# Tile starts rounded to 256 bytes, an earlier first unit, and a per-unit norm with its root on GpSimd

## The chip, the core and the metric

One core of a Trainium2 chip runs the program. TensorE (PE in the profile) multiplies matrices and loads its weights under the row name PEld; VectorE is DVE, ScalarE is ACT, GpSimd is POOL, and SyncE (SP) issues most transfers. The metric is device time in microseconds (us), the median of several executions.

## The reference, cut to what matters

```
for c in range(nc):                      # 24 chunks of 32 positions
    L = exp(cum[:, :, :, None] - cum[:, :, None, :]) * causal
    y[:, :, sl] = einsum(M = CB * L, xc) + einsum(Cc, state) * exp(cum)
    state = decay_full * state + sum(Bx)
x = y as 3072 tokens x 256
xn = x / sqrt(mean(x * x) + 1e-6) * rms_g
x = (silu(xn @ w_gate) * (xn @ w_val)) @ w_out      # 256 -> 1536 -> 256
return softplus(x @ w_in) @ w_out2                  # 256 -> 2048 -> 256
```

A decaying scan over the sequence (4 batches, 8 heads) is followed by a norm and two MLP layers, all in float32.

## The kernel before, in words

The 3072 tokens are 24 units of 128 tokens, and four units make one of six blocks of 512 tokens. A **unit** is the scan part: the decay factors of its tokens are spread over partitions, DVE scans them (line 502), PE makes scores (`a<-hw` in the first eight units), DVE multiplies the two (line 549), PE makes the unit's output (`t<-xc`, `t<-ab,xc`), and ACT stores its square and its copy scaled by `rms_g` in the tiles `xxh` and `xxl`. For the first four units the spread is two matmuls for each half of a unit, with the identity as weights (`p<-Sm,ident`; `Sm` there holds the clipped factors); later units fetch a spread copy by DMA (`ab<-a_clip`). The **norm** of a block sums squares on PE (`p<-mean,xxh`), takes the inverse root on DVE by three Newton steps (lines 628 to 637), spreads it over partitions on PE (`p<-ident,rs`), multiplies on DVE (line 656), and splits the product into a float32r high part (ACT, line 299) and a rest (DVE, line 306). `NORMS = {0: [3, 1]}` says that block 0 does this for units 0 to 2 together and for unit 3 alone.

The **MLP** then takes each product in three passes, high weight by high input, high by rest and rest by high, with 512 columns a matmul. Layer 1 has F1 = 12 tiles of 128 and 18 matmuls in each, layer 2 has F2 = 16 tiles and 12 in each, so a block takes 12 x 18 + 16 x 12 = 408 such matmuls and the six blocks 2448. Their weights (`wgh` to `wpl`) stay in SBUF; their moving operand is in an `xx` tile, an `hw` tile, or, for the first two tiles of layer 1 in blocks 3 to 5 (`EARLY`), in a `wr` tile. Weights arrive in 34 chunks in three `wr` buffers and are turned into pairs by ACT and DVE (lines 386 to 393); the first three chunks are issued on ACT's queue, the others on SP's.

**Fillers** are 40 matmuls of a constant (`p<-mean`, both operands read with a step of zero) that do no work for the result. Eight of them come first by rank, and 32 have the last rank of all, so they stand wherever the planner sees PE idle.

The order of each engine is set by `Plan.emit`: every operation has a rank, an estimated duration and its dependences, and the planner picks at each step the operation that can start first, by rank among equals. An engine then runs its instructions in that order, and an instruction that waits holds up those behind it.

SBUF tiles are placed one behind another, in steps of 32 bytes. Because `cst_sb` has 257 columns and `wr` has 1025, the starts are not multiples of 256 bytes. In the built program the start modulo 256 is 224 for all ten weight tiles; 64 for `xx`, `hw`, `s`, `ab` and `xc`; 192 for `cz` and `st`; and 224, 0 and 32 for the three `wr` buffers.

Of the kernel before, what the change touches and what calls it, by code (L numbers as in the profile page):

```python
# [17 lines left out]
P = 128  # L18
# [6 lines left out]
BLOCKS = [4, 4, 4, 4, 4, 4]  # L25

NATIVE, SPREAD = 8, 4
NORMS = {0: [3, 1]}

EARLY, HEAD = 2, 2  # L30

# [203 lines left out]
def tile_ssd_then_swiglu_then_softplus_mlp(  # L235
# [75 lines left out]
        plan.op({"sp": (kb * 4.0, fn)}, rank, r, w)  # L311


    cst_sb = const.tile([P, DM + 1], F32, name="cst_sb")
    ident4 = const.tile([P, 4 * P], F32, name="ident4")
    ident = ident4[:, 0:P]
    mask = cst_sb[:, 0:DM]
    zeros = cst_sb[:, DM:DM + 1].to_broadcast([P, P])
    g_sb = const.tile([P, KD], F32, name="g_sb")
    cz = [const.tile([P, 4, 2, P], F32, name=f"cz{i}") for i in range(2)]  # L320
    mean = const.tile([P, 1], F32, name="mean")
    zz = [const.tile([P, 4 * P], F32, name=f"zz{i}") for i in range(2)]


# [42 lines left out]
    def weight(c):  # L367
        nm, i = chunks[c]
        b0 = blocks[0]
        use = b0["t1"] + 2 * i * b0["d1"] if nm in ("wg", "wv", "wo") else b0["t2"] + 2 * i * b0["d2"]  # L370
        if nm in ("wo", "wp"):
            use += 2.0
        rank = use - W_LEAD

        raw = buf("wr", [P, 8 * P + 1], I32, N_W)
        mid = lambda: raw()[:, 1:].rearrange("p (n j) -> p n j", j=2)[:, :, 0]
        r = lambda: mid().bitcast(F32)

        plan.op({"actq" if c < N_W else "sp": (512 * 4.0, lambda: (act if c < N_W else nc.sync).dma_start(
            out=raw().bitcast(U16)[:, 1:-1], in_=w[c].bitcast(U16)))}, -150 + c if c < N_W else rank, (), [raw])  # L380
        n = 2 * KD * P

        z, zk = zz[c % 2], ("zz", c % 2)
        ACT(n, rank, lambda: act.activation(out=z.bitcast(F16).rearrange("p (n j) -> p n j", j=2)[:, :, 1],
            in_=raw().bitcast(BF16)[:, 2:].rearrange("p (n j) -> p n j", j=4)[:, :, 2], func=ACTF.Copy, scale=0.5), [raw], [zk])
        DVE(n, rank, lambda: dve.scalar_tensor_tensor(out=mid(), in0=mid(), scalar=13, in1=z.bitcast(I32),  # L388
            op0=ALU.logical_shift_right, op1=ALU.bitwise_or), [raw, zk], [raw])
# [12 lines left out]
        COPY(n, rank, lambda: l, gp, [gp], [(nm, i, 1)], False)
# [20 lines left out]
    def split(t):  # L423
        rank = base_of(NB * t) - B_LEAD
        for q in range(2):
            hl = buf("wr", [P, 8 * P + 1], I32, N_W)
            hi, lo = (lambda hl=hl, k=k: f32(hl()[:, 4 * P * k:4 * P * (k + 1)]) for k in range(2))
            LOAD(256, rank, lambda q=q, lo=lo: nc.sync.dma_start(out=lo(), in_=bc[t, :, q]), [hl])
            ACT(512, rank, lambda hi=hi, lo=lo: act.activation(out=hi().bitcast(F32R), in_=lo(), func=ACTF.Copy), [hl], [(hl, 0)])
            DVE(512, rank, lambda hi=hi, lo=lo: dve.tensor_tensor(out=lo().bitcast(F32R), in0=lo(), in1=hi(), op=ALU.subtract),  # L430
                [hl, (hl, 0)], [hl])
            for i, (p, k, sl) in enumerate(((hi, (hl, 0), slice(0, 4, 2)), (lo, hl, slice(1, 4, 2))) if q == 0 else
                                           ((hi, (hl, 0), slice(0, 2)), (lo, hl, slice(2, 4)))):
                LOAD(512, rank, lambda p=p, q=q, sl=sl: nc.sync.dma_start(
                    out=parts[t][q][:, sl], in_=p().rearrange("p (o f) -> p o f", o=1).to_broadcast([P, 2, 4 * P])),
                    [("parts", t, 2 * q + i)], [k])

    def unit(u):
# [87 lines left out]
        if nat:  # L526

            def scores():
                for q in range(4):
                    c = slice(q * P, (q + 1) * P)  # L530
                    for z in range(2):
                        rows = slice(r0 + 64 * z, r0 + 64 * z + NS)
                        mm(gps[z]()[:, c], bct()[rows, 0, c], bct()[rows, 1, c], True, True)
            PE(1100, rank[0], scores, [(bct, b % 2, 0), (bct, b % 2, 1)], list(gps), 512)
        else:
            def pairs():
                for q in range(4):
# [73 lines left out]
    def norm(t, o0, nu, rank, step):  # L611

        c = slice(o0 * P, (o0 + nu) * P)
        sq, y, r0 = ysq[t]
        ss, rs = buf("ss", [P, 4], F32, 2), buf("rs", [P, 2, 4], F32, 2)
        nb = pbuf("a" if t else "p", [P, 4 * P])

        def msum():
# [2 lines left out]
                    mm(nb()[:, o:o + 1], sq()[:, k, (o0 + o) * P:(o0 + o + 1) * P], mean, k == 0, k == KD - 1)  # L621
        PE(230 * KD * nu, rank, msum, [(sq, o0 + o) for o in range(nu)] + ["mean"], [nb], 8)

        def root():


            r, q, m = rs()[:, 0, 0:nu], rs()[:, 1, 0:nu], ss()[:, 0:nu]
            dve.tensor_scalar(out=m, in0=nb()[:, 0:nu], scalar1=1e-6, scalar2=0.5, op0=ALU.add, op1=ALU.mult)
            dve.tensor_scalar(out=r.bitcast(I32), in0=m.bitcast(I32), scalar1=-0.5, scalar2=float(0x5F3759DF - 2 ** 22 - 2 ** 31),
                              op0=ALU.mult, op1=ALU.add)  # L630
            for _ in range(3):
                if nu == 1:
                    dve.scalar_tensor_tensor(out=q, in0=r, scalar=r, in1=m, op0=ALU.mult, op1=ALU.mult)
                else:
                    dve.tensor_tensor(out=q, in0=r, in1=r, op=ALU.mult)
                    dve.tensor_tensor(out=q, in0=q, in1=m, op=ALU.mult)
                dve.scalar_tensor_tensor(out=r, in0=q, scalar=1.5, in1=r, op0=ALU.subtract, op1=ALU.mult)
        DVE(0, rank + step, root, [nb, "mean"], [rs, ss], port=False, ns=(8 if nu == 1 else 11) * 185)

        def spread():  # L640
            for o in range(nu):
                mm(nb()[:, o * P:(o + 1) * P], rs()[:, 0, o:o + 1].to_broadcast([P, P]), ident, True, True)
        PE(240 * nu, rank + step, spread, [rs, "ident"], [nb], 512 * nu)
        if not o0:
            xnT[t] = [buf(f"xx{k}", [P, KD, 4 * P], F32R, 3) for k in "hl"]
# [3 lines left out]
            h.rank = l.rank = r0 + 0.01  # L649

        for ks in ([slice(0, KD)] if nu < 4 else [slice(k, k + 1) for k in range(KD)]):
            m = ks.stop - ks.start
            n = m * nu * P
            yk = [(y, k, o0 + o) for o in range(nu) for k in range(ks.start, ks.stop)]
            hv, lv, yv = (lambda b=b, ks=ks: b()[:, ks, c] for b in (h, l, y))
            DVE(n, rank + 2 * step, lambda yv=yv, m=m: dve.tensor_tensor(out=yv(), in0=yv(), in1=nb()[:, 0:nu * P].rearrange(
                "p (o i) -> p o i", o=1).to_broadcast([P, m, nu * P]), op=ALU.mult), yk + [nb], yk, port=False)
            COPY(n, rank + 2 * step, hv, yv, yk, [(h, o0, ks.start)])
            REST(n, rank + 2 * step, lv, yv, hv, yk + [(h, o0, ks.start)], [(l, o0, ks.start)])
            xkeys.setdefault(t, []).extend([(h, o0, ks.start), (l, o0, ks.start)])  # L660
# [16 lines left out]

    def split_h(key, s, n, rank, early=False):
        if early:
            hhl = buf("wr", [P, 8 * P + 1], I32, N_W)  # L680
            hhl.view = lambda t: t[:, 0:8 * P].bitcast(F32R).rearrange("p (s i) -> p s i", s=2)
        else:
            hhl = buf("hw", [P, 2, 4 * P], F32R, N_H)
# [72 lines left out]
    with tc.manual_schedule():  # L756
# [14 lines left out]
        LOAD(96, -101, lambda: nc.sync.dma_start(out=a_sb(), in_=a_view(ab)), [a_sb])  # L771
        DVE(384, -101, clip_all, [a_sb], [a_sb])
        LOAD(96, -101, lambda: nc.sync.dma_start(out=a_view(a_clip), in_=a_sb()), ["a_clip"], [a_sb])
        LOAD(128, -10, lambda: nc.sync.dma_start(out=cst_sb, in_=cst), ["cst"], ["a_clip"])
        LOAD(20, -1, lambda: nc.sync.dma_start(out=g_sb, in_=rms_g), ["g"])
        DVE(1, -104, lambda: dve.memset(mean, 1.0 / DM), (), ["mean"])
        for i in range(2):
            POOL(500, -103, lambda i=i: pool.memset(zz[i], 0.0), (), [("zz", i)])
        for i in range(2):
# [111 lines left out]
```

## Time and profile before

| what | value |
|---|---|
| median of 3 runs | 677.12 us (676.54 to 677.94) |
| time of the profiled execution | 677.4 us |
| its span, first to last instruction | 675.5 us |
| PE busy | 665.6 us, 99% |
| DVE busy | 343.9 us, 51% |
| ACT busy | 308.4 us, 46% |
| POOL busy | 20.6 us, 3% |

A busy PE is not a PE at its peak, because matmuls overlap and the end of each is modelled; the distance from one start to the next tells more. Some 1.9 us of the execution lie outside the span.

### The profile page before, as it was taken

How to read it: one execution, taken by the hardware profiler on the slowest of the kernel's cores; microseconds unless marked ns; L12 is line 12 of the kernel's file. 1: busy time of each engine (PE TensorE's matmuls, PEld its weight loads, DVE VectorE, ACT ScalarE, POOL GpSimd, SP SyncE). 2: the span in 40 equal slices, each digit the busy share in tenths (PEclk: the TensorE clock that was granted, in tenths of full speed). 3: DMA queues.
4: the chain of work that ended last, by engine and by line, in shares of the span. 5: the costliest groups of instructions: out<-in, count | busy, mean ns of one | idle time of the engine just before them, and what ended most of it. 6: DMA issues, size and time to landing. Idle time of an engine off the chain costs nothing.

```text
span 675.5 us, 9002 instructions
## 1 busy us (share of the span) xinstructions
PE 665.6 (99%) x3492; PEld 533.5 (79%) x3492; DVE 343.9 (51%) x580; ACT 308.4 (46%) x541; POOL 20.6 (3%) x28
## 2 busy tenths in 40 slices
PE   7999999999999999999999999999999999999997
PEld 5677788888888888888888888888888888887785
DVE  2969898785862226763423873433653422233321
ACT  3247756775444445332644432544432544422543
POOL 1000000000000000000000100000100000000000
PEclk9989999999999999999999999999999999999999
DMA  6746677555620006120231620040500000000000
GB/s 200 212 128 224 228 264 233 202 188 175 190 57 32 0 1 190 57 67 0 83 120 37 210 67 1 30 167 7 194 1 1 0 1 0 32 0 1 0 1 31
DMA packets 36777, 61.36 MB, mean 91 GB/s; under 512 B 3424, under 2 KB 18304, under 8 KB 36736
## 3 DMA queue, kind: packets, MB, share of 16 engines
q1 hardware_dynamic: 36304, 59.23, 27.0%
q10 hardware_dynamic: 432, 1.57, 0.7%
q8 instruction: 27, 0.44, 0.3%
q14 instruction: 14, 0.11, 0.1%
HBM read 47.58 MB, written 13.21 MB: 90 GB/s over the span
## 4 chain that ended last, share of the span: by engine, by line
PE 95%; DMA 2%; DVE 1%; issue 1%; ACT 0%; SPq 0%; DVEq 0%
PE p L268 52%; PE t L268 35%; PE a L268 7%; DMA ab<-a_clip 1%; DMA hw<-in_bc 1%; DVE ab L502 0%; DVE hw L306 0%; ACT hw L299 0%; DVE ab L549 0%; DVE xxh L549 0%; DVE s L793 0%; DVE xxl L746 0%; DVE s L705 0%; DVE wr L388 0%; ACT s L717 0%
## 5 line engine op out<-in xcount | busy, mean ns | idle before, releaser
L306 DVE TENSOR_TENSOR hw<-s,hw 128x512 fp32r<-128x512 f32 x162 | 113.4, 702 | 187.3 <-ACT hw L299 186.8
L299 ACT ACTIVATE hw<-s 128x512 fp32r<-128x512 f32 x162 | 101.8, 631 | 113.7 <-DVE s L705 87.1
L268 PE MATMUL t<-hw,wph 128*128 128x512 f32 x384 | 121.2, 396 | 0.2 <-DVE hw L306 0.2
L717 ACT ACTIVATE s<-p 128x512 f32<-128x512 f32 x96 | 57.0, 599 | 109.0 <-PE p L268 108.1
L705 DVE TENSOR_TENSOR s<-s,p 128x512 f32<-128x512 f32 x72 | 49.2, 684 | 79.8 <-PE p L268 71.2
L268 PEld LDWEIGHTS t<-hw,wph 128*128 128x128 f32 x384 | 71.3, 188 | 19.0 <-issue 1.2
L268 PE MATMUL t<-hw,woh 128*128 128x512 f32 x264 | 83.6, 397 | 0.3 <-DVE hw L306 0.2
L268 PE MATMUL p<-xxh,wil 128*128 128x512 f32 x192 | 76.5, 399 | 0.0
L268 PE MATMUL t<-hw,wpl 128*128 128x512 f32 x192 | 76.5, 398 | 0.0
L268 PE MATMUL p<-xxl,wih 128*128 128x512 f32 x192 | 75.8, 395 | 0.2 <-DVE xxl L746 0.2
L268 PE MATMUL p<-xxh,wih 128*128 128x512 f32 x192 | 75.5, 393 | 0.0
L701 ACT ACTIVATE s<-p 128x512 f32<-128x512 f32 x72 | 43.0, 597 | 57.3 <-PE p L268 56.5
L268 PEld LDWEIGHTS t<-hw,woh 128*128 128x128 f32 x264 | 49.0, 188 | 13.2 <-ACT hw L299 0.6
L268 PE MATMUL p<-xxh,wgh 128*128 128x512 f32 x144 | 57.5, 399 | 0.0
L268 PE MATMUL p<-xxh,wvl 128*128 128x512 f32 x144 | 57.3, 398 | 0.0
L268 PE MATMUL p<-xxh,wgl 128*128 128x512 f32 x144 | 57.2, 398 | 0.0
L268 PE MATMUL p<-xxh,wvh 128*128 128x512 f32 x144 | 57.1, 397 | 0.0
L268 PE MATMUL p<-xxl,wgh 128*128 128x512 f32 x144 | 56.9, 395 | 0.0
L268 PE MATMUL p<-xxl,wvh 128*128 128x512 f32 x144 | 56.8, 395 | 0.0
L502 DVE TENSOR_TENSOR_SCAN ab<-ab,ident 128x512 f32<-128x512 f32 x40 | 50.3, 1277 | 5.1 <-DMA ab<-a_clip 4.9
L268 PE MATMUL t<-hw,wol 128*128 128x512 f32 x132 | 52.5, 398 | 0.0
L268 PEld LDWEIGHTS p<-xxl,wih 128*128 128x128 f32 x192 | 36.0, 188 | 9.7 <-DVE xxl L746 0.7
(120 smaller groups left out, 791.3 us busy)
## 6 DMA issues: line engine op xcount, KB each, us to landing
wr<-in_w SPq DMA_DIRECT2D x31, 512.0 KB, 3.3
ab<-a_clip SPq DMA_DIRECT2D x20, 512.0 KB, 4.2
parts<-wr SPq DMA_DIRECT2D x16, 512.0 KB, 3.5
xc<-in_xc SPq DMA_DIRECT2D x20, 256.0 KB, 4.2
st<-parts SPq DMA_DIRECT2D x16, 256.0 KB, 3.3
cz<-parts SPq DMA_DIRECT2D x32, 128.0 KB, 3.6
out_y<-s SPq DMA_DIRECT2D x12, 256.0 KB, 3.8
wr<-in_bc SPq DMA_DIRECT2D x8, 256.0 KB, 3.0
```

Source lines behind the costliest of these rows:

```text
L268: pe.matmul(out=o, lhsT=l, rhs=r, start=start, stop=stop, skip_group_check=True)
L299: ways = {"act": (act_ns(n), lambda: act.activation(out=out(), in_=in_(), func=ACTF.Copy)), "dve": (dve_ns(n, sbuf), lambda: dve.tensor_co ...
L306: return lambda: eng.tensor_tensor(out=out(), in0=in_(), in1=f32(hi()), op=ALU.subtract)
L502: DVE(512, rank[0], lambda t=t, d=d: dve.tensor_tensor_scan(out=t(), data0=d(), data1=ident4, initial=0.0, op0=ALU.mult, op1=ALU.add), dk ...
L701: ACT(n, rank - EPI, lambda: act.activation(out=s()[:, 0:n], in_=ps[0]()[:, 0:n], func=ACTF.Silu), [ps[0]], [s, "table"] if new_table else ...
L705: DVE(n, rank - EPI, lambda: dve.tensor_tensor(out=s()[:, 0:n], in0=s()[:, 0:n], in1=ps[1]()[:, 0:n], op=ALU.mult), [s, ps[1]], [s], port= ...
L717: ACT(n, rank - EPI, lambda: act.activation(out=s()[:, 0:n], in_=hp()[:, 0:n], func=ACTF.Softplus), [hp], [s, "table"] if new_table and f ...
```

## The change

Four things are changed. (1) Tiles get sizes that keep every large tile's start at a multiple of 256 bytes: `cst_sb` is padded, the small constants share a tile or get 64 columns, and `wr` has 8P + 64 columns in place of 8P + 1. In the built program the start modulo 256 is 0 for every tile of weights, `xx`, `hw`, `wr`, `s`, `ab`, `xc`, `cz` and `st`. (2) The first three weight loads depend on `ident`, so that ACT issues them behind its first copies. (3) The scores of the first four units depend on `a_sb`, the clipped factors. (4) The norm of block 0 goes unit by unit, and its root is one ACT copy that adds 1e-6 and one power of -0.5 on POOL in place of the Newton steps on DVE; the other blocks keep the Newton steps.

```diff
-NORMS = {0: [3, 1]}
+NORMS = {0: [1, 1, 1, 1]}
...
-    cst_sb = const.tile([P, DM + 1], F32, name="cst_sb")
+    sbuf_at = 1152
+    cst_sb = const.tile([P, -(-(sbuf_at // 4 + DM + 1) // 64) * 64 - sbuf_at // 4], F32, name="cst_sb")
...
-    g_sb = const.tile([P, KD], F32, name="g_sb")
+    small = const.tile([P, 64], F32, name="small")
+    g_sb, mhalf = small[:, 0:KD], small[:, KD:KD + 1]
+    mean = const.tile([P, 64], F32, name="mean")[:, 0:1]
...
-    mean = const.tile([P, 1], F32, name="mean")
...
-        raw = buf("wr", [P, 8 * P + 1], I32, N_W)
+        raw = buf("wr", [P, 8 * P + 64], I32, N_W)
...
-            out=raw().bitcast(U16)[:, 1:-1], in_=w[c].bitcast(U16)))}, -150 + c if c < N_W else rank, (), [raw])
+            out=raw().bitcast(U16)[:, 1:16 * P + 1], in_=w[c].bitcast(U16)))}, -150 + c if c < N_W else rank, ["ident"] * (c < N_W), [raw])
...
-            PE(1100, rank[0], scores, [(bct, b % 2, 0), (bct, b % 2, 1)], list(gps), 512)
+            PE(1100, rank[0], scores, [(bct, b % 2, 0), (bct, b % 2, 1)] + [a_sb] * (u < SPREAD), list(gps), 512)
...
-        ss, rs = buf("ss", [P, 4], F32, 2), buf("rs", [P, 2, 4], F32, 2)
+        rs = buf("rs", [P, 64], F32, 2)
...
+        r, q, m = (lambda i=i: rs()[:, 4 * i:4 * i + nu] for i in range(3))
+        if t == 0:
+
+            ACT(nu, rank, lambda: act.activation(out=m(), in_=nb()[:, 0:nu], func=ACTF.Copy, bias=1e-6), [nb], [rs])
+            POOL(150, rank, lambda: pool.tensor_tensor(out=r(), in0=m(), in1=mhalf.to_broadcast([P, nu]), op=ALU.pow), [rs, "mhalf"], [rs])
+        else:
+            def root():
...
+            DVE(0, rank + step, root, [nb, "mean"], [rs], port=False, ns=11 * 195)
...
+        DVE(1, -101, lambda: dve.memset(mhalf, -0.5), (), ["mhalf"])
```

`split` and `split_h` take the same wider `wr` tile, and the rest of the diff renames.

PE's order at the start of the program, before (`hw` holds the inputs of the scores, `Sm` the clipped factors, `mean` the fillers):

```order
L268 MATMUL p<-mean 128x512 x8
L268 MATMUL a<-hw 128x128 x8
L268 MATMUL p<-Sm,ident_68 128x256 x12
L268 MATMUL t<-xc 32x64 x4
L268 MATMUL t<-ab,xc 32x128 x8
```

The same place now:

```order
L268 MATMUL p<-mean 128x512 x10
L268 MATMUL p<-Sm,ident_68 128x256 x4
L268 MATMUL a<-hw 128x128 x8
L268 MATMUL p<-Sm,ident_68 128x256 x4
L268 MATMUL p<-mean 128x512 x17
L268 MATMUL t<-xc 32x64 x4
L268 MATMUL t<-ab,xc 32x128 x8
```

The spreads of unit 0 moved ahead of its scores, those of unit 2 moved behind unit 0's output, and 17 fillers now stand between the spreads of unit 1 and the output of unit 0. In both programs the same 176 matmuls, all 40 fillers among them, stand ahead of the first MLP matmul.

DVE's order at the start, before (the scan is named SCALAR_TENSOR_TENSOR here; `wr<-wr,zz` is a step of a weight chunk):

```order
L770 MEMSET Sm 96x2
L388 SCALAR_TENSOR_TENSOR wr<-wr,zz_73 128x512
L502 SCALAR_TENSOR_TENSOR ab<-p,ident_68 128x512
L388 SCALAR_TENSOR_TENSOR wr<-wr,zz_74 128x512
L502 SCALAR_TENSOR_TENSOR ab<-p,ident_68 128x512
L791 TENSOR_SCALAR s<-s 96x256
```

The same place now:

```order
L775 MEMSET Sm 96x2
L505 SCALAR_TENSOR_TENSOR ab<-p,ident_68 128x512 x2
L391 SCALAR_TENSOR_TENSOR wr<-wr,zz_73 128x512
L525 TENSOR_TENSOR xc<-xc,ab 128x128
L505 SCALAR_TENSOR_TENSOR ab<-p,ident_68 128x512
L552 TENSOR_TENSOR ab<-ab,a 128x512
```

The first weight chunk's step moved from ahead of the first scan to behind the second.

POOL's order now, from its first work on block 0 (`rs<-rs,small` is the power, `Sm<-S,cst_sb` the masked state that stood alone there before):

```order
L786 MEMSET cz_71 128x1024
L786 MEMSET cz_72 128x1024
L631 ISA
L631 TENSOR_TENSOR rs<-rs,small 128x1 x2
L515 TENSOR_TENSOR Sm<-S,cst_sb 128x256
L631 TENSOR_TENSOR rs<-rs,small 128x1 x2
```

Four powers came to POOL, and the 19 small DVE instructions of the two roots of block 0 (11 and 8) are gone from DVE.

## Rows read from the trace of the kernel before

**Rows 1.** The page: busy time of the engines.

```profile
PE 665.6 (99%) x3492; PEld 533.5 (79%) x3492; DVE 343.9 (51%) x580; ACT 308.4 (46%) x541; POOL 20.6 (3%) x28
```

**Rows 2.** Waits of PE, 47 to 675.5 us: total, times, longest.

```profile
PE t L268 <- DVE hw L306: 0.4, 2, 0.2
```

**Rows 3.** The chain of work that ended last: start, us, what.

```profile
322.42 9.80 PE p L268 x42
```

**Rows 4.** Timeline of PE, 0 to 20 us: start, us, what, [idle before].

```profile
0.92 3.78 PE L268 MATMUL p<-mean 128*128 128x512 f32 x8 [0.92 <-DVE mean L776]
7.47 0.79 PE L268 MATMUL a<-hw 16*128 16x128 f32 x2 [2.77 <-DMA hw<-in_bc]
8.78 2.07 PE L268 MATMUL a<-hw 16*128 16x128 f32 x14 [0.52 <-DMA hw<-in_bc]
10.78 8.64 PE L268 MATMUL p<-Sm,ident 96*128 96x256 f32 x24
```

**Rows 5.** Timeline of DVE, 5 to 47 us.

```profile
5.31 0.29 DVE L769 TENSOR_SCALAR Sm<-Sm 96x256 f32<-96x256 f32 x1 [4.45 <-DMA Sm<-in_ab]
5.73 0.69 DVE L388 SCALAR_TENSOR_TENSOR wr<-wr,zz 128x512 int32<-128x512 int32 x1
12.89 1.22 DVE L502 TENSOR_TENSOR_SCAN ab<-p,ident 128x512 f32<-128x512 f32 x1 [6.47 <-PE p L268]
...
28.02 1.23 DVE L502 TENSOR_TENSOR_SCAN ab<-ab,ident 128x512 f32<-128x512 f32 x1 [0.81 <-DMA ab<-a_clip]
...
34.89 0.15 DVE L628 TENSOR_SCALAR ss<-p 128x3 f32<-128x3 f32 x1
...
36.92 0.68 DVE L549 TENSOR_TENSOR xxl<-xxl,a 128x512 f32<-128x512 f32 x1
...
39.02 0.95 DVE L656 TENSOR_TENSOR xxl<-xxl,p 128x768 f32<-128x768 f32 x1 [1.02 <-PE p L268]
40.72 0.69 DVE L549 TENSOR_TENSOR ab<-ab,a 128x512 f32<-128x512 f32 x1 [0.74 <-PE a L268]
...
42.19 0.15 DVE L628 TENSOR_SCALAR ss<-p 128x1 f32<-128x1 f32 x1
...
43.80 0.68 DVE L549 TENSOR_TENSOR ab<-ab,a 128x512 f32<-128x512 f32 x1
45.28 0.42 DVE L656 TENSOR_TENSOR xxl<-xxl,p 128x256 f32<-128x256 f32 x1 [0.80 <-PE p L268]
46.18 0.62 DVE L306 TENSOR_TENSOR xxl<-xxl,xxh 128x256 fp32r<-128x256 f32 x1 [0.48 <-ACT xxh L299]
```

**Rows 6.** Timeline of PE: later fillers, and the first MLP matmul.

```profile
26.46 2.89 PE L268 MATMUL p<-mean 128*128 128x512 f32 x12
...
47.21 0.40 PE L268 MATMUL p<-xxh,wgh 128*128 128x512 f32 x1
```

**Rows 7.** Timeline of PE, 471 to 586 us: MLP matmuls from two kinds of tile.

```profile
471.68 0.40 PE L268 MATMUL p<-xxl,wih 128*128 128x512 f32 x1
471.92 0.39 PE L268 MATMUL p<-xxh,wil 128*128 128x512 f32 x1
...
477.34 0.62 PE L268 MATMUL t<-wr,woh 128*128 128x512 f32 x2
...
478.03 0.62 PE L268 MATMUL t<-wr,woh 128*128 128x512 f32 x2
...
478.71 0.63 PE L268 MATMUL t<-wr,woh 128*128 128x512 f32 x2
...
583.94 0.63 PE L268 MATMUL t<-wr,woh 128*128 128x512 f32 x2
...
585.33 0.40 PE L268 MATMUL p<-xxh,wgh 128*128 128x512 f32 x1
```

**Rows 8.** Timeline of POOL, 0 to 50 us.

```profile
0.24 0.10 POOL L834 MEMSET const-float32-0.0<- 128x1 f32 x1 [0.24 <-issue]
...
24.02 0.73 POOL L512 TENSOR_TENSOR Sm<-S,cst_sb 128x256 f32<-128x256 f32 x1 [20.52 <-PE p L268]
```

More of the change, by code (lines that the diff above doesn't have):

```diff
@@ L373, in weight @@
         rank = use - W_LEAD
-        raw = buf("wr", [P, 8 * P + 1], I32, N_W)
-        mid = lambda: raw()[:, 1:].rearrange("p (n j) -> p n j", j=2)[:, :, 0]
+        raw = buf("wr", [P, 8 * P + 64], I32, N_W)
+        mid = lambda: raw()[:, 1:8 * P + 1].rearrange("p (n j) -> p n j", j=2)[:, :, 0]
         r = lambda: mid().bitcast(F32)
         plan.op({"actq" if c < N_W else "sp": (512 * 4.0, lambda: (act if c < N_W else nc.sync).dma_start(
-            out=raw().bitcast(U16)[:, 1:-1], in_=w[c].bitcast(U16)))}, -150 + c if c < N_W else rank, (), [raw])
+            out=raw().bitcast(U16)[:, 1:16 * P + 1], in_=w[c].bitcast(U16)))}, -150 + c if c < N_W else rank, ["ident"] * (c < N_W), [raw])
         n = 2 * KD * P
@@ L386, in weight @@
         ACT(n, rank, lambda: act.activation(out=z.bitcast(F16).rearrange("p (n j) -> p n j", j=2)[:, :, 1],
-            in_=raw().bitcast(BF16)[:, 2:].rearrange("p (n j) -> p n j", j=4)[:, :, 2], func=ACTF.Copy, scale=0.5), [raw], [zk])
+            in_=raw().bitcast(BF16)[:, 2:16 * P + 2].rearrange("p (n j) -> p n j", j=4)[:, :, 2], func=ACTF.Copy, scale=0.5), [raw], [zk])
         DVE(n, rank, lambda: dve.scalar_tensor_tensor(out=mid(), in0=mid(), scalar=13, in1=z.bitcast(I32),
@@ L425, in split @@
         for q in range(2):
-            hl = buf("wr", [P, 8 * P + 1], I32, N_W)
+            hl = buf("wr", [P, 8 * P + 64], I32, N_W)
             hi, lo = (lambda hl=hl, k=k: f32(hl()[:, 4 * P * k:4 * P * (k + 1)]) for k in range(2))
@@ L622, in norm @@
         PE(230 * KD * nu, rank, msum, [(sq, o0 + o) for o in range(nu)] + ["mean"], [nb], 8)
[L624 to L637, printed above, removed]
@@ L638, in norm @@
-        DVE(0, rank + step, root, [nb, "mean"], [rs, ss], port=False, ns=(8 if nu == 1 else 11) * 185)
+        r, q, m = (lambda i=i: rs()[:, 4 * i:4 * i + nu] for i in range(3))
[4 more added lines that the diff above has]
+            def root():
+                dve.tensor_scalar(out=m(), in0=nb()[:, 0:nu], scalar1=1e-6, scalar2=0.5, op0=ALU.add, op1=ALU.mult)
+                dve.tensor_scalar(out=r().bitcast(I32), in0=m().bitcast(I32), scalar1=-0.5,
+                                  scalar2=float(0x5F3759DF - 2 ** 22 - 2 ** 31), op0=ALU.mult, op1=ALU.add)
+                for _ in range(3):
+                    dve.tensor_tensor(out=q(), in0=r(), in1=r(), op=ALU.mult)
+                    dve.tensor_tensor(out=q(), in0=q(), in1=m(), op=ALU.mult)
+                    dve.scalar_tensor_tensor(out=r(), in0=q(), scalar=1.5, in1=r(), op0=ALU.subtract, op1=ALU.mult)
+            DVE(0, rank + step, root, [nb, "mean"], [rs], port=False, ns=11 * 195)
@@ L640, in spread @@
         def spread():
             for o in range(nu):
-                mm(nb()[:, o * P:(o + 1) * P], rs()[:, 0, o:o + 1].to_broadcast([P, P]), ident, True, True)
+                mm(nb()[:, o * P:(o + 1) * P], r()[:, o:o + 1].to_broadcast([P, P]), ident, True, True)
         PE(240 * nu, rank + step, spread, [rs, "ident"], [nb], 512 * nu)
@@ L651, in norm @@
         for ks in ([slice(0, KD)] if nu < 4 else [slice(k, k + 1) for k in range(KD)]):
-            m = ks.stop - ks.start
-            n = m * nu * P
+            nk = ks.stop - ks.start
+            n = nk * nu * P
             yk = [(y, k, o0 + o) for o in range(nu) for k in range(ks.start, ks.stop)]
             hv, lv, yv = (lambda b=b, ks=ks: b()[:, ks, c] for b in (h, l, y))
-            DVE(n, rank + 2 * step, lambda yv=yv, m=m: dve.tensor_tensor(out=yv(), in0=yv(), in1=nb()[:, 0:nu * P].rearrange(
-                "p (o i) -> p o i", o=1).to_broadcast([P, m, nu * P]), op=ALU.mult), yk + [nb], yk, port=False)
+            DVE(n, rank + 2 * step, lambda yv=yv, nk=nk: dve.tensor_tensor(out=yv(), in0=yv(), in1=nb()[:, 0:nu * P].rearrange(
+                "p (o i) -> p o i", o=1).to_broadcast([P, nk, nu * P]), op=ALU.mult), yk + [nb], yk, port=False)
             COPY(n, rank + 2 * step, hv, yv, yk, [(h, o0, ks.start)])
@@ L679, in split_h @@
         if early:
-            hhl = buf("wr", [P, 8 * P + 1], I32, N_W)
+            hhl = buf("wr", [P, 8 * P + 64], I32, N_W)
             hhl.view = lambda t: t[:, 0:8 * P].bitcast(F32R).rearrange("p (s i) -> p s i", s=2)
@@ L773, in tile_ssd_then_swiglu_then_softplus_mlp @@
         LOAD(96, -101, lambda: nc.sync.dma_start(out=a_view(a_clip), in_=a_sb()), ["a_clip"], [a_sb])
-        LOAD(128, -10, lambda: nc.sync.dma_start(out=cst_sb, in_=cst), ["cst"], ["a_clip"])
+        LOAD(128, -10, lambda: nc.sync.dma_start(out=cst_sb[:, 0:DM + 1], in_=cst), ["cst"], ["a_clip"])
         LOAD(20, -1, lambda: nc.sync.dma_start(out=g_sb, in_=rms_g), ["g"])
         DVE(1, -104, lambda: dve.memset(mean, 1.0 / DM), (), ["mean"])
+        DVE(1, -101, lambda: dve.memset(mhalf, -0.5), (), ["mhalf"])
         for i in range(2):
```

## The prediction, as it stood before the result

> **What bounds the kernel now.** I read the page's busy line first, then PE's waits, then the chain. PE is busy 99% of the span and no other engine much over half [rows 1]. From 47 us to the end PE waits for others well under 1 us; the largest entry is 0.4 us [rows 2]. So after the start the time is the number of matmuls times the distance between them. The chain gives that distance: 42 MLP matmuls in 9.80 us, 0.2333 us each [rows 3]. 2448 of them make 571 us. Before the first of them, at 47.21 us [rows 6], PE's busy time means little, since fillers pad it. There DVE sets the pace: its first scan starts at 12.89 us after a wait of 6.47 us for PE, and from there to the end of the last rest at 46.80 us it is held up five times, for 0.81, 1.02, 0.74, 0.80 and 0.48 us, 3.85 us in all [rows 5]. PE takes up the first MLP matmul 0.41 us after that last rest. So two things can change the time: when DVE ends its part of the start, and the distance between MLP matmuls.
>
> **The start.** The scan of unit 0 needs its spread. Before, PE made eight fillers, stood idle 2.77 us for the scores' inputs, did the scores, and began the spreads at 10.78 us [rows 4]; the scan followed 2.1 us behind. The clipped factors, all that the spread needs beside the identity, were ready at 5.73 us, where DVE turned to a weight chunk [rows 5]. Now the spreads stand ahead of the scores. Ten fillers take 10/8 of 3.78 us and end at about 5.6 us, so the spread starts near 5.75 and the first scan at 5.75 + 2.1 = 7.85 us, **5.0 us earlier**. The transfers of 1.5 MB of weights that ran beside the clipped factors' load now come later, which may bring that load forward; I take nothing for it.
>
> From the first scan on, DVE has the same work but for these: the two roots go, 34.89 to 36.92 us and 42.19 to 43.80 us, **3.64 us** [rows 5]. The first weight step, 0.69 us, moves in from a time when DVE was idle. Four multiplies of 0.42 us replace 0.95 + 0.42, which adds 0.31 us, and four rests of 0.62 us replace 0.95 + 0.62, which adds 0.91 us (taking the 256-column rows for each). Together 33.91 - 3.64 + 0.69 + 0.31 + 0.91 = 32.2 us if DVE is held up for 3.85 us as before, and 28.3 us if never. DVE then ends at 40.0 or 36.2 us and the first MLP matmul comes at 40.4 or 36.6 us, 6.8 or 10.6 us earlier.
>
> What may be late instead: the weights now wait for `ident`, and DVE's third work item is the step on their first chunk. The wait has cover, for two scans of 1.22 us stand before it. The other is PE: 17 fillers stand between the spreads of unit 1 and the output of unit 0, and behind them the scores of unit 1, which DVE's multiplies wait for. At the speed of the early fillers (8 in 3.78 us, the lower clock level of 1.2 GHz after an idle start) 17 take 8.0 us, at that of the later ones (12 in 2.89 us, the level of 2.4 GHz) 4.1 us [rows 4, 6]. The 24 spreads before took 8.64 us, and PE had been idle for 2.77 and 0.52 us shortly before them. Now it has no such gap, so I expect the higher level earlier than before, but with 3.9 us between the two cases I take a good part of the old waits as kept. I take the first MLP matmul at 39.2 us, **8.0 us earlier**, between 4 us (late fillers on top of the old waits) and 10.6 us (no wait).
>
> **The root on POOL.** No row shows a power. Its cost lies between POOL's 0.10 us for one column and 0.73 us for 256 columns of two inputs [rows 8]; I take the upper, since a power is more work than a multiply. Before, 3.09 us passed from unit 3's root to its multiply, 1.61 of them the root; the new chain is about 1.5 + 0.73 + 0.4 for ACT's copy, 2.6 us. Between unit 3's last score product and its multiply DVE now has another multiply, two scans, two products and a rest, over 5 us by the rows above. So it costs nothing; without that cover it would cost up to 2.6 us, four times at worst for the four units. Nothing past the first MLP matmul changes in count: the same 176 matmuls stand ahead of it.
>
> **The alignment.** All weights lay at 224 modulo 256, nearly all moving operands at 64, and now both lie at 0. The trace of before holds one natural trial: tiles of `wr`. With the moving operand in the `wr` buffer at 224, the same remainder as the weights, six matmuls from 477.34 to 478.71 us take 1.37 us, 0.2283 each, and six from 583.94 to 585.33 take 1.39 us, 0.2317 each [rows 7]. The mean is 0.2300 us against 0.2333. From 478.03 to 478.71 three even take 0.2267 us each. So the distance does depend on where operands lie, and equal remainders are the quicker case. 2448 x 0.0033 us is **8.2 us**. The bounds: all at 0.2267 us give 16.3 us; none, if it was the `wr` place and not its remainder. A quicker PE asks more of DVE, but that is busy half the time on the whole; I take nothing off.
>
> The Trainium skill speaks against this term: its page "SBUF — State Buffer", in the section on Door 1, tells of lines of 16 bytes, within which accesses run at full bandwidth and between which each crossing pays. All starts before were already multiples of 32, so by that rule rounding them to 256 gives nothing, and the sum would hold the start alone. The twelve matmuls above do not agree with it.
>
> **The sum.** The profiled execution took 677.4 us, 0.3 us over the median of the runs. 677.4 - 8.0 - 8.2 = 661.2; I forecast **661 us**. About 0.2%, or 1.4 us, is what a measurement of this kernel can tell from no change.
>
> **Rivals.** (B) *Alignment does nothing.* The quick `wr` stretches are short, and `wr` also lies elsewhere in SBUF; the distance stays 0.2333 us and only the start is gained: 677.4 - 8.0 = 669.4 us. For it: only twelve matmuls speak against it. Against it: 42 matmuls in a row keep to 0.2333 us, while these twelve do not. The rule of the Trainium skill's page "SBUF — State Buffer" above would give this time too.
>
> (C) *Equal remainders make the streams collide, and the time is longer.* Weights for the next matmul are read while the present one's operand streams; with everything at 0 the two may meet more often. Single distances of 0.24 us occur already (471.68 to 471.92 us [rows 7]); were all such, 2448 x 0.0067 = 16.3 us would be added: 677.4 - 8.0 + 16.3 = 685.7 us. It decides from 0.2366 us a matmul on, where it eats the start's 8.0 us. Against it: equal remainders in the `wr` rows were quicker.
>
> (E) *The start gives nothing.* PE runs its 17 fillers at the lower level, DVE waits for scores and for weight chunks, and what the earlier scan wins is lost at the products of unit 1; with the distance unchanged the time is 677 us. For it: PE's queue is in order, so a filler that is wrongly placed delays the output behind it. Against it: all of 5.0 + 3.64 us would have to be lost.
>
> **How the numbers follow.** My case holds 0.65, B 0.20, C 0.09, E 0.06. The range runs from both gains at their bounds, 677.4 - 10.6 - 16.3 = 650.5, to the least start gain with no gain of distance, 677.4 - 4 = 673.4: 650 to 673 us. It leaves out C, E, and 0.05 of my own case for a distance under 0.2267 us, 0.20 in all. Faster by over 0.2%: 0.60 + 0.05 + 0.20 = 0.85. Within 0.2%: 0.04 of E. Slower: 0.09 of C and 0.02 of E, 0.11.
>
> **What the new profile would show.** The first scan near 7.9 us, not 12.9; the first MLP matmul between 36.6 and 43 us; no Newton steps on DVE before it; and pieces of the chain in which 42 MLP matmuls take 9.66 us, not 9.80. The prediction is wrong if those 42 still take 9.80 us (B) or over 9.9 (C), if DVE's first multiplies by scores wait several us for PE (E), or if, with a quicker PE, waits for DVE appear in the MLP part where there was 0.4 us before.

## The result, and the profile after

| | before | after |
|---|---|---|
| median | 676.83 us, 4 executions, those shown and one more (676.46 to 677.94) | 652.78 us, 4 executions (651.48 to 662.91) |
| profiled execution, its span | 677.4, 675.5 us | 651.5, 649.0 us |
| first MLP matmul | 47.21 us | 34.99 us |
| from there to the end of the span | 628.3 us | 614.0 us |
| 42 MLP matmuls | 9.80 us | 9.52 us |

The ratio of the times is 0.9636, with a 95% interval of 0.9615 to 0.9656. Executions over 1.5% above the fastest of their kernel, here the one of 662.91 us with a mean granted clock of TensorE of 0.986 in place of 1.0, are left out of the ratios. The forecast was 661 us, in a range of 650 to 673. The profiled executions differ by 25.9 us: 12.2 us in the start and 14.3 us behind the first MLP matmul, less 0.6 us outside the span. The profiled execution is the fastest of the four; the next two took 1.3 us more.

The page's busy line, and PE's waits from 36 us to the end (total us, times, longest us), answer to [rows 1, 2]:

```profile
PE 643.7 (99%) x3492; PEld 528.9 (81%) x3492; DVE 339.7 (52%) x566; ACT 309.9 (48%) x547; POOL 24.6 (4%) x32
```

```profile
PE t L268 <- DVE hw L306: 0.5, 2, 0.2
PE p L268 <- DVE xxl L751: 0.2, 1, 0.2
PE t L268 <- ACT hw L299: 0.2, 1, 0.2
```

PE still bounds the kernel, and a quicker PE brought no new wait. The chain (start, us, what) has pieces of 42 matmuls as in [rows 3]; three of them stand in it, each of 9.52 us:

```profile
304.40 9.52 PE p L268 x42
```

That is 0.2267 us each, against 0.2333. PE's timeline (start, us, what, idle before) answers to [rows 4, 6]:

```profile
0.92 4.19 PE L268 MATMUL p<-mean 128*128 128x512 f32 x10 [0.92 <-DVE small L782]
4.95 1.89 PE L268 MATMUL p<-Sm,ident 96*128 96x256 f32 x8
6.77 1.16 PE L268 MATMUL a<-hw 16*128 16x128 f32 x16
...
9.50 4.07 PE L268 MATMUL p<-mean 128*128 128x512 f32 x17
...
16.18 1.97 PE L268 MATMUL p<-Sm,ident 96*128 96x256 f32 x8
17.99 0.39 PE L268 MATMUL p<-ident,rs 128*128 128x128 f32 x2
...
34.99 0.40 PE L268 MATMUL p<-xxh,wgh 128*128 128x512 f32 x1
```

The spreads no longer stand behind a wait for the scores' inputs. The 17 fillers take 0.24 us each, like the twelve in [rows 6]; the first ten take 0.42 us each, near the 0.47 of the eight in [rows 4]. The prediction called that slow pace the 1.2 GHz level. The granted clock doesn't show it: it reads 1.00, which is 2.4 GHz, from 0 to 6 us in both profiles, so what makes the first fillers slow is not shown. DVE's timeline answers to [rows 5]:

```profile
3.67 0.29 DVE L774 TENSOR_SCALAR Sm<-Sm 96x256 f32<-96x256 f32 x1 [2.77 <-DMA Sm<-in_ab]
...
6.08 2.34 DVE L505 TENSOR_TENSOR_SCAN ab<-p,ident 128x512 f32<-128x512 f32 x2 [1.99 <-issue]
...
14.76 0.29 DVE L797 TENSOR_SCALAR s<-s 96x256 f32<-96x256 f32 x1 [1.33 <-DMA s<-in_ab]
...
34.29 0.41 DVE L306 TENSOR_TENSOR xxl<-xxl,xxh 128x256 fp32r<-128x256 f32 x1
```

The first scan starts 6.81 us earlier, the factors were there at 3.67 us in place of 5.31, and from the first scan to the last rest only one wait is over 0.2 us: 1.33 us for a transfer (`s`, a second copy of the decay factors). There are no Newton steps. Of POOL's rows, which answer to [rows 8], these are the four powers:

```profile
17.23 0.55 POOL L631 TENSOR_TENSOR rs<-rs,small 128x1 f32<-128x1 f32 x1 [13.73 <-ACT rs L630]
20.97 0.56 POOL L631 TENSOR_TENSOR rs<-rs,small 128x1 f32<-128x1 f32 x1 [3.18 <-ACT rs L630]
...
25.40 0.92 POOL L631 TENSOR_TENSOR rs<-rs,small 128x1 f32<-128x1 f32 x1 [2.06 <-ACT rs L630]
30.44 0.75 POOL L631 TENSOR_TENSOR rs<-rs,small 128x1 f32<-128x1 f32 x1 [4.12 <-ACT rs L630]
```

In PE's timeline unit 0's root is spread at 17.99 us with no wait: the spreads `p<-Sm,ident` of 1.97 us stand between it and the sum of squares, and cover the copy and the power.

### The profile page after: what moved, and what is told of

It reads as the page before. It is cut to its first block, busy times and chain, and to the rows that moved or that the text cites. A ratio compares the mean times of both kernels' runs of the same rounds, so it can differ in the third digit from the quotient of the medians.

```text
span 649.0 us, 9018 instructions
## 1 busy us (share of the span) xinstructions
PE 643.7 (99%) x3492; PEld 528.9 (81%) x3492; DVE 339.7 (52%) x566; ACT 309.9 (48%) x547; POOL 24.6 (4%) x32
## 4 chain that ended last, share of the span: by engine, by line
PE 98%; ACT 0%; DVE 0%; issue 0%; DVEq 0%
PE p L268 55%; PE t L268 36%; PE a L268 8%; DVE hw L306 0%; ACT hw L299 0%; DVE xxl L751 0%; DVE s L710 0%; ACT s L722 0%; ACT xxh L299 0%; ACT s L756 0%; DVE mean L781 0%; DVE small L782 0%; DVEq L710 0%
## 5 line engine op out<-in xcount | busy, mean ns | idle before, releaser
L268 PE MATMUL t<-hw,wph 128*128 128x512 f32 x384 | 119.6, 392 | 0.2 <-DVE hw L306 0.2
L268 PE MATMUL t<-hw,woh 128*128 128x512 f32 x264 | 82.3, 392 | 0.4 <-DVE hw L306 0.2
L268 PE MATMUL t<-hw,wpl 128*128 128x512 f32 x192 | 74.7, 389 | 0.0
L268 PE MATMUL p<-xxh,wil 128*128 128x512 f32 x192 | 74.7, 389 | 0.0
```

What stands on the lines that cost most here:

```text
L268: pe.matmul(out=o, lhsT=l, rhs=r, start=start, stop=stop, skip_group_check=True)
```

## The experiments

Twelve kernels in three groups, each with the kernel before run beside it: its median was 677.48 us in the first group (e1 to e4), 677.14 in the second (e5 to e8) and 676.62 in the third (e9 to e12).

### What in the alignment counts: e1, e3, e4, e6, e9

**e1** is the kernel before with part (1) alone, the tile sizes; the order of PE is that of before.

```diff
-    cst_sb = const.tile([P, DM + 1], F32, name="cst_sb")
+    sbuf_at = 1152
+    cst_sb = const.tile([P, -(-(sbuf_at // 4 + DM + 1) // 64) * 64 - sbuf_at // 4], F32, name="cst_sb")
...
-        raw = buf("wr", [P, 8 * P + 1], I32, N_W)
+        raw = buf("wr", [P, 8 * P + 64], I32, N_W)
...
```

> The kernel before with only the tile starts of the change (weights and moving operands at 0 modulo 256); its order, norm and weight loads stay as before, so PE's instructions stand in the same order. In the changed kernel the first MLP matmul starts 12.2 us earlier (34.99 against 47.21) and 42 MLP matmuls take 9.52 us against 9.80. If the tile starts alone give the second part, this run has 42 matmuls in 9.52 us, a first MLP matmul still near 47 us, and about 677 - 14 = 663 us in all. If the shorter distance came with the new order (other work beside the matmuls), it stays at 9.80 and the time near 677.

Measured: 661.51 us, ratio 0.9753 (0.972 to 0.9787), 42 matmuls in 9.52 us, the first MLP matmul at 45.72 us and 613.9 us from there to the end of its span of 659.6 us. The alignment alone gives 16.0 us, 14.4 of them behind the first MLP matmul: as much as the whole change has there. One of the pieces in e1's chain:

```profile
418.00 9.52 PE p L268 x42
```

**e3, e6, e9** put a pad ahead of the weight tiles and the rest of 256 bytes behind them, so that weights start at 32, 64 or 128 modulo 256 and moving operands stay at 0. **e4** has only the first pad, so weights and moving operands are all at 32. The columns of the two pads are 8 and 56 in e3 (shown), 16 and 48 in e6, 32 and 32 in e9.

```diff
+    const.tile([P, 8], F32, name="pad0")
...
+    const.tile([P, 56], F32, name="pad1")
```

> The changed kernel with 32 bytes ahead of the weight tiles and 224 behind them: weights at 32, moving operands at 0. Theory 1 (the difference of the two starts counts): 42 MLP matmuls take 9.80 us and the time is near 667 us. Theory 2 (the weights' own start counts, as a multiple of 64): also 9.80. Theory 3 (only the moving operand's own start counts, as a multiple of 256): 9.52 us and 652 us.

> The changed kernel with 32 bytes ahead of the weight tiles and nothing behind: weights and moving operands all at 32. Theory 1 (the difference counts): 42 MLP matmuls take 9.52 us and the time stays near 652 us, though no start is a multiple of 64. Theory 2 (the weights' own start) and theory 3 (the moving operand's own start): 9.80 us and about 667 us.

> The changed kernel with every weight tile's start at 64 modulo 256 and every moving operand's at 0, so the difference of the starts is 64. Theory 1a (what counts is the difference of the two starts modulo 64): 42 MLP matmuls take 9.52 us and the time is near 652 us if the start runs as in the changed kernel. Theory 1b (the difference counts modulo a larger number, 128 or 256): 9.80 us, or something between, and a time near 668 us.

> The changed kernel with every weight tile's start at 128 modulo 256 and every moving operand's at 0. A difference of 32 or 64 gave 9.80 us for 42 MLP matmuls, a difference of 0 gave 9.52. Theory 1b (the difference counts modulo 256): 9.80 us. Theory 1c (it counts modulo 128): 9.52 us.

One execution each. The same piece of the chain in e3, e4, e6 and e9, in this order:

```profile
531.12 9.80 PE p L268 x42
```

```profile
510.83 9.52 PE p L268 x42
```

```profile
530.69 9.80 PE p L268 x42
```

```profile
520.66 9.76 PE p L268 x42
```

Each chain has three such pieces, of the same length. All at 32 is as quick as all at 0 (e4: 652.91 us), so no start has to be a multiple of 256 or even of 64. Weights 32, 64 or 128 away from the moving operand are slow (e3 676.5, e6 676.36, e9 665.84 us). What counts is the **difference** of the two starts. It is not taken modulo 64 or 128, since 64 and 128 are slow, 128 by a hair less than the others (9.76 us). Of e3's and e6's times some 10 us are a bad start, one in which PE waits for unit 0's root and its clock falls (below), and the 42 matmuls are the reading that counts.

### The start: e2, e7, e5, e8, e10, e11, e12

**e2** is the other half, the changed kernel with the tile sizes of before (part (1) of the diff reversed).

> The changed kernel with the tile sizes of before, so that weights start at 224 and moving operands at 64 modulo 256 again; order, loads and norm as changed. If the two parts add up, the first MLP matmul stays near 35 us, 42 matmuls take 9.80 us again, and the time is about 677 - 12 = 665 us. If the alignment also made the start shorter, the first MLP matmul comes later than 35 us by the missing part and the time is over 667 us.

Measured: 672.25 us (ten executions, 666.56 to 676.85), ratio 0.9905 (0.9871 to 0.9939), 42 matmuls in 9.80 us. The profiled one took 673.14 us, with the first MLP matmul at 42.09 us. Its chain:

```profile
422.86 9.80 PE p L268 x42
```

So the start alone gives 5.2 us in the median of the ten and 10.9 in the best. What the others lose shows in e6, which has the changed order too, with the first MLP matmul at 45.23 us. DVE's, ACT's and PE's timelines of e6:

```profile
17.05 0.29 DVE L799 TENSOR_SCALAR s<-s 96x256 f32<-96x256 f32 x1 [3.36 <-DMA s<-in_ab]
...
18.03 0.66 DVE L393 SCALAR_TENSOR_TENSOR wr<-wr,zz 128x512 int32<-128x512 int32 x1
```

```profile
18.73 0.66 ACT L396 ACTIVATE woh<-wr 128x512 fp32r<-128x512 f32 x1 [2.71 <-DVE wr L393]
19.30 0.15 ACT L632 ACTIVATE rs<-p 128x1 f32<-128x1 f32 x1
```

```profile
15.90 1.97 PE L268 MATMUL p<-Sm,ident 96*128 96x256 f32 x8
20.13 0.49 PE L268 MATMUL p<-ident,rs 128*128 128x128 f32 x2 [2.26 <-POOL rs L633]
...
24.27 3.76 PE L268 MATMUL p<-Sm,ident 96*128 96x256 f32 x8
```

The transfer of `s` (line 794 of the changed kernel) lands late, DVE runs in order and waits 3.36 us for it, the third weight step behind it is late, ACT's copy `woh` waits for that step, and ACT's root copy of unit 0 stands behind `woh`. PE waits 2.26 us for the power, and afterwards unit 3's eight spreads take 3.76 us where unit 2's took 1.97. The windows view of e6 (window, its length, busy time and instructions of PE, PEld, DVE, ACT, POOL, then the granted clock, DMA share, GB/s) has the clock at its lower level, 1.2 GHz, from then on for several stretches:

```profile
12.00:18.00 6.00, 5.88 (x60) 4.50 (x59) 2.60 (x7) 2.17 (x6) 0.00 (x0) 1.00 0.31 88
18.00:24.00 6.00, 3.87 (x45) 3.18 (x46) 5.15 (x9) 2.12 (x7) 0.55 (x1) 0.75 0.87 209
24.00:30.00 6.00, 6.00 (x40) 4.64 (x41) 4.27 (x8) 0.42 (x3) 1.27 (x2) 0.50 1.05 351
30.00:36.00 6.00, 6.00 (x30) 5.14 (x28) 2.56 (x4) 1.24 (x5) 0.55 (x1) 0.50 0.10 32
```

In e2 the same three waits are 4.22, 1.22 and 2.58 us. Part of the lateness can be read from SyncE's queue, of the changed kernel and of e2:

```profile
4.61 1.90 SPq L475 DMA_DIRECT2D hw<-in_bc  x2
6.62 0.35 SPq L778 DMA_DIRECT2D a_clip<-Sm  x1
...
12.53 0.43 SPq L794 DMA_DIRECT2D s<-in_ab  x1
```

```profile
4.84 3.61 SPq L474 DMA_DIRECT2D hw<-in_bc  x2
8.57 0.35 SPq L777 DMA_DIRECT2D a_clip<-Sm  x1
...
14.55 0.43 SPq L793 DMA_DIRECT2D s<-in_ab  x1
```

Two issues of score inputs take 1.90 us in one and 3.61 in the other, and all behind them, the write of the clipped factors and `s` among it, comes 2.0 us later. That is half of it: DVE has `s` at 18.71 us in place of 14.76, 3.95 us later, so the transfer itself took longer too. The same two issues take 2.18 us in e4 and 1.97 in e9, where DVE waits under 2 us for `s`, and 2.84 in e3, 2.83 in e6 and 3.76 in e8 (below), where it waits 3.36 us or more. Why they take longer in some executions is open.

The tile starts may have a part in it: e2 came out as the second case of its expectation, in which the alignment also shortens the start. Of the kernels with the changed order, those whose weights and moving operands have the same remainder (the changed kernel, e4, and e5 and e7 below) kept a mean granted clock of at least 0.997 in 12 of 13 executions; those with unequal remainders (e2, e3, e6, e9) did in 3 of 13. Equal remainders are no guarantee, since e8's profiled execution has the late `s` too. So e2 may well understate what the start gives in the changed kernel; no run tests why.

**e5** issues `s` third on that queue, and drops its dependence on the clipped copy, which it doesn't read. The order on every other engine stays.

```diff
-        LOAD(96, 10, lambda: nc.sync.dma_start(out=p_sb(), in_=a_view(ab)), [p_sb], ["a_clip"])
+        LOAD(96, -100.5, lambda: nc.sync.dma_start(out=p_sb(), in_=a_view(ab)), [p_sb])
```

> The changed kernel with one transfer moved: the second copy of the decay factors (s from in_ab, 96x256) is SyncE's third transfer in place of about its fourteenth, and reads in_ab without waiting for the clipped copy. The order on every other engine is the same. Theory 1 (in some executions that transfer lands late, DVE waits for it, the third weight step and behind it ACT's root copy come late, PE stands idle 2.6 us for unit 0's root and its clock falls): every execution now starts alike, DVE waits under 0.3 us for s, the first MLP matmul comes at 34 to 35.5 us, the clock stays at the full level, the runs lie within 0.3% of each other and the median is 650 to 652 us. Theory 2 (the spread has nothing to do with that transfer): some executions are still 1.5% longer, with a granted clock near 0.986. Theory 3 (the earlier transfer delays the clipped factors or the scores' inputs on SyncE's queue): the first scan comes 0.3 to 1 us later than 6.08 us and the time is 652 to 654 us.

Measured: 653.04 us (four executions, 652.36 to 653.98, granted clock 0.998 to 1.0), ratio 0.9643 (0.9628 to 0.9658). The wait for `s` is gone (DVE waits 1.10 us for the constants `cst_sb` behind it instead) and the clock stays up, as theory 1 has it; but the first MLP matmul is at 35.88 us in the profiled execution, its slowest, and the median isn't better than the changed kernel's, so its number fell. Theory 3's numbers hold, not its mechanism: the first scan is 0.9 us later at 6.97 us, though the factors landed at 3.81 us, for PE's ten first fillers took 4.63 us in place of 4.19. They took 3.92 in e6 and e9 and 4.60 in e7, none of which has the early transfer, so this varies by itself. That the early `s` makes a bad start rarer fits e5's four executions; four are too few to show it.

**e7** undoes part (2).

```diff
-            out=raw().bitcast(U16)[:, 1:16 * P + 1], in_=w[c].bitcast(U16)))}, -150 + c if c < N_W else rank, ["ident"] * (c < N_W), [raw])
+            out=raw().bitcast(U16)[:, 1:16 * P + 1], in_=w[c].bitcast(U16)))}, -150 + c if c < N_W else rank, (), [raw])
```

> The changed kernel with part (2) undone: the first three weight loads no longer depend on the identity and are issued on ACT's queue at once. The order on PE up to the first MLP matmul differs by fillers alone. Theory 1 (the weight transfers beside the clipped factors' load delay it, which is why it landed at 3.67 us in the changed kernel and at 5.31 us before): the factors land near 5.3 us again, the first scan comes at 7.3 to 7.8 us, the first MLP matmul 1 to 2 us later than 34.99, and the time is 0.5 to 2 us over the changed kernel's. Theory 2 (the earlier landing has another reason): factors at 3.7 us, first scan at 6.1 us, time as in the changed kernel within 0.3%.

Measured: 653.48 us (653.09 to 655.1), ratio 0.9657 (0.9637 to 0.9676). DVE takes up the factors at 5.31 us again, to the hundredth the time of [rows 5], and the first scan is at 6.95 us, earlier than theory 1's 7.3 to 7.8, the first MLP matmul at 36.88. So the three weight loads do delay the factors by 1.6 us, but the ten fillers end at 5.5 us and hide most of it. On the median it is 0.7 us, and the intervals of the two ratios overlap, so part (2) has no gain that these runs can tell.

**e8** undoes part (4); **e10** does so with e5's early `s`, since e8's DVE waited 3.53 us for `s`.

```diff
-NORMS = {0: [1, 1, 1, 1]}
+NORMS = {0: [3, 1]}
...
-        if t == 0:
+        if t < 0:
```

> The changed kernel with part (4) undone: block 0's norm goes for units 0 to 2 together and unit 3 alone, with Newton steps on DVE. All else, the tile starts too, is the changed kernel's, except that the planner puts the fillers elsewhere. Theory 1 (DVE sets the pace of the start, and the roots' 3.6 us come off it): DVE has 3.64 us more in roots and 1.2 us less in small multiplies and rests, so the first MLP matmul comes 2 to 3.5 us later, 37 to 38.5 us, and the time is 654 to 656 us; no wait of PE for POOL. Theory 2 (the new norm gives nothing in the start, since DVE has idle time there to hold the roots): the first MLP matmul at 34.5 to 35.5 us and the changed kernel's time within 0.3%.

> The early transfer of s together with block 0's norm as it was before (units 0 to 2 together, unit 3 alone, Newton steps on DVE). It takes the late s, which cost e8_norm_undone a wait of 3.53 us on DVE and a fall of the clock, out of the comparison; it is held against e5_early_ab. Theory 1 (the new norm saves DVE's 3.64 us of roots and most of that reaches the first MLP matmul): no wait over 1.5 us for s, the first MLP matmul at 38 to 39.5 us against 35.88, and 655 to 657 us. Theory 2 (what e8_norm_undone lost came from the late s alone): the first MLP matmul within 1 us of 35.88 and the time within 0.3% of 653.0 us.

Measured: e8 660.06 us (657.5 to 664.1), ratio 0.9751 (0.9712 to 0.979), first MLP matmul at 43.13 us. e10 657.28 us (656.6 to 659.24), ratio 0.9713 (0.9693 to 0.9733), first MLP matmul at 39.41 us. Against e5 the old norm costs 4.2 us of the median and 3.5 us of the first MLP matmul, about the roots' 3.64 us (e5 and e10 to e12 are of two groups, whose medians of before lie 0.5 us apart). DVE's wait for the last spread is the one over 1 us behind its first scan in e10:

```profile
37.33 0.42 DVE L661 TENSOR_TENSOR xxl<-xxl,p 128x256 f32<-128x256 f32 x1 [2.38 <-PE p L268]
```

That spread stands on PE behind six weight matmuls, most of them at 1.2 GHz: the granted clock was 0.50 from 30 to 36 us (`p<-wr,wil` x2 took 1.91 us at 32.42, 1.07 at 37.06), although PE had had no wait over 0.35 us since its first matmul. So not all of the 4.2 us is root.

**e11** has e5's early `s` and the unit-by-unit norm, with each root by Newton steps on DVE (`if t < 0` alone).

> The early transfer of s, block 0's norm unit by unit as in the changed kernel, but each root by Newton steps on DVE, 11 small instructions in place of ACT's copy and POOL's power. Theory 1 (the root on GpSimd is hidden and DVE sets the pace): four roots add about 8 us of small instructions to DVE (before, two took 3.64 us), the first MLP matmul comes 4 to 8 us later than 35.88, at 40 to 44 us, and the time is 657 to 661 us. Theory 2 (DVE has idle time to hold them): within 1.5 us of 35.88 and within 0.3% of 653.0 us.

Measured: 663.00 us (662.15 to 663.53), ratio 0.9788 (0.9772 to 0.9805), first MLP matmul at 46.60 us, 10.7 us later than e5. It is theory 1, and dearer than it said. Unit 2's root on PE and DVE in e11:

```profile
32.08 0.15 DVE L636 TENSOR_SCALAR rs<-p 128x1 f32<-128x1 f32 x1
...
34.00 0.16 DVE L642 SCALAR_TENSOR_TENSOR rs<-rs 128x1 f32<-128x1 f32 x1
```

```profile
29.96 0.61 PE L268 MATMUL p<-mean,xxh 128*128 128x1 f32 x4
34.21 0.80 PE L268 MATMUL p<-ident,rs 128*128 128x128 f32 x2 [3.65 <-DVE rs L642]
...
39.05 2.05 PE L268 MATMUL p<-wr,wil 128*128 128x512 f32 x2
```

A root takes DVE 2.08 us, four 8.3 us. The sum of squares ends near 30.6 us, but on DVE the root stands behind a scan and a product and ends at 34.16; PE, in order, stands idle 3.65 us, and its clock falls (granted 0.50 from 33 to 42 us, weight matmuls of 2.05 us a pair). Unit by unit with its roots on DVE, the norm is slower than the old norm of e10; it pays only because its root left DVE.

**e12** undoes part (3), with e5's early `s`.

```diff
-            PE(1100, rank[0], scores, [(bct, b % 2, 0), (bct, b % 2, 1)] + [a_sb] * (u < SPREAD), list(gps), 512)
+            PE(1100, rank[0], scores, [(bct, b % 2, 0), (bct, b % 2, 1)], list(gps), 512)
```

> The early transfer of s with part (3) undone: the scores of the first four units no longer depend on the clipped factors, so unit 0's scores stand ahead of its spreads again on PE, behind nine fillers; the planner also moves 13 of the fillers. Theory 1 (the order of scores and spreads gave 2 us or more of the earlier first scan, since PE waits for the scores' inputs first): PE waits 2 to 3 us for hw behind the fillers, the first scan comes at 8.5 to 11 us, the first MLP matmul at 37.5 to 40 us, and the time is 654.5 to 657 us. Theory 2 (the inputs of the scores now land early enough, so the order is worth only the scores' own 1.2 us): first scan 7 to 8.3 us, first MLP matmul 36 to 37.5 us, and the time within 0.3% of 653.0 us.

Measured: 664.39 us (663.78 to 668.92), ratio 0.9828 (0.9793 to 0.9862). The first scan is at 10.58 us, as theory 1 has it, but the first MLP matmul at 48.06 us and the time are beyond both theories. PE's timeline of e12:

```profile
6.41 2.07 PE L268 MATMUL a<-hw 16*128 16x128 f32 x14 [0.56 <-DMA hw<-in_bc]
8.40 6.36 PE L268 MATMUL p<-Sm,ident 96*128 96x256 f32 x16
...
18.13 0.42 PE L268 MATMUL t<-ab,xc 128*32 128x128 f32 x8 [1.40 <-DVE ab L552]
19.84 0.43 PE L268 MATMUL t<-ab,xc 128*32 128x128 f32 x8 [1.29 <-DVE ab L552]
...
23.59 3.76 PE L268 MATMUL p<-Sm,ident 96*128 96x256 f32 x8
```

PE waited 0.56 us for inputs, not 2 to 3, but scores and spreads ran slowly (sixteen spreads in 6.36 us, at a granted clock of 1.00), PE then waited 2.7 us for DVE's products, and the next spreads took 3.76 us, at 0.50. A first scan 3.6 us later became 11.4 us of time: the rest is PE waiting for DVE, a lower clock, and DVE waiting for spreads (2.44 us at 25.68). But the planner set more than the scores elsewhere: fillers moved, and DVE now turns to `s` ahead of unit 1's scans and waits there 1.74 us, to 15.44, for the constants `cst_sb`. So how much of the 11.4 us is the scores' dependence as such is not shown.

## Why the prediction was right, and where it was off

**What bounds the kernel** held: PE 99% busy, no new wait in the MLP part, 176 matmuls ahead of the first MLP matmul. The time is the sum of a start and of distances: e1's 16.0 us and e2's 5.2 us (median) to 10.9 (best execution) hold the 24.1 us between them. The medians alone make 21.2, so the two parts are not shown to add cleanly.

**The alignment** was the right mechanism, undersized. I took 0.2300 us, the mean of twelve matmuls from the `wr` buffer at 224, and 8.2 us. The distance is 0.2267, the lower bound, for which I had three matmuls; by 42 in a row that would be 16.3 us, and e1 measured 14.4 behind the first MLP matmul, 5.9 ns a matmul in place of 6.7. Longer single distances are still there in other stretches of the changed kernel (its PE timeline has 0.24 us from 465.95 to 466.19 us), and what sets them I did not follow up.

The reason that I gave for the quick `wr` stretches, equal remainders, is what e3, e4, e6 and e9 show, and of the two common remainders tried, 0 and 32, neither is better. Rivals B and C fell with e1. The 16-byte rule of the Trainium skill's page "SBUF — State Buffer" (section on Door 1) says nothing against a second effect, but it doesn't give it: all starts of e3, e6 and e9 are multiples of 32, and their 42 matmuls take 9.76 to 9.80 us against 9.52.

**The start** was forecast 8.0 us shorter, 10.6 at most, and is 12.2 in the profiled execution. The step that failed by size is the sum up to the first MLP matmul. I had the first scan at 7.85 us and it was at 6.08, 1.8 us better: the spread began at 4.95 us, not 5.75, since the fillers took less than 10/8 of 3.78 us, and the scan followed it by 1.1 us, not 2.1, since eight spreads took 1.89 us in place of a third of 8.64. That the factors came earlier too, for which I took nothing, was right to leave out (e7). From the first scan to the first MLP matmul I had 31.4 us and it was 28.9, 2.4 us better: of the old waits, kept in good part, one of 1.33 us was left, and a rest of 256 columns took 0.41 us, not the 0.62 of [rows 5].

Both errors lie on the same side, so the result is 8 us under the forecast, near the lower end of the range. The start passed its bound by 1.6 us; that the time is inside the range all the same is in part luck, since the distances gave 14.3 us and not the 16.3 of theirs.

**The root on POOL** cost nothing in the profiled execution, and the power's price of 0.73 us lies inside the 0.55 to 0.92 measured. But I looked for its cover only in DVE's work, and only for unit 3. Its weak place is unit 0: ACT's queue has a weight copy ahead of the root copy, and when that is late PE waits 2.26 us (e6) or 2.58 (e2). This comes near rival E, which had DVE wait for weight chunks; here DVE waited for `s`, and a weight chunk waited behind it. It put the first MLP matmul 7 us (e2) to 10 us (e6) later than in the changed kernel. Rival E as a whole fell. Whether the changed kernel's execution of 662.91 us lost its time there is not shown, since its trace is of another execution.

What I priced too low is how the pieces hang together. By their own prices the roots were worth 3.64 us and the scores' order 5.0; undone one at a time from e5 they cost 4.2 and 11.4 us, and roots on DVE unit by unit 10.0. Together the first two are more than the whole gain of the start, so the pieces don't add. In all three runs the clock fell as well: in e11 and e12 behind a wait of PE, in e10 without one. How much of each cost is the clock no run separates.

## What to carry to other kernels

Read the distance between matmuls from an undisturbed piece of the chain, not from busy time: 0.28 us in 42 matmuls was 14.4 us behind the start of e1, and it came from the placement of tiles alone. Give weights and moving operands starts with the same remainder modulo 256; here 0 and 32 served alike. In a short start on one in-order PE queue, price a late piece by the wait that it gives PE and by a fall of the clock, not by its own microseconds alone, and look on each queue (SyncE's issues, ACT's copies) for what stands ahead of the late one.

## What the runs showed of the hardware that was not expected

The distance of matmuls of 512 float32r columns depends on the difference of the operands' starts modulo 256: 0.2267 us at 0 (changed kernel, e1, e4, e5, e7, e8, e10 to e12), 0.2333 at 32, 64 and, before, 160; 0.2324 at 128 (e9). Why is open; other differences were not tried by themselves.

TensorE's granted clock fell where PE had waited 2.26 us (e6) or 3.65 us (e11), but a long wait isn't needed. In e9 the longest wait of PE after its first matmul was 0.31 us, at 18.19 us, and the clock still fell for a while. In the windows of e9 (columns as above) PE is busy nearly all the time:

```profile
12.00:18.00 6.00, 5.88 (x60) 4.50 (x59) 4.03 (x10) 2.45 (x7) 0.41 (x1) 1.00 0.44 128
18.00:24.00 6.00, 5.81 (x54) 4.75 (x55) 5.54 (x8) 1.60 (x6) 0.69 (x2) 0.75 0.94 260
24.00:30.00 6.00, 6.00 (x77) 4.89 (x79) 5.45 (x10) 1.90 (x7) 1.27 (x2) 0.96 0.86 279
```

In e10 and e9, then, PE's waits don't account for the fall; what in its work does, no run here tells. A power of one column took POOL 0.55, 0.56, 0.75 and 0.92 us for the same work.
